# Interleaving the last recurrent segment with four gate/up products, moving weight loads to GpSimd's queue, and three small edits upstream

One Trainium2 chip, one core. The metric is the device time of one execution in microseconds, lower is better; medians of several runs are quoted. The page of a profile describes one execution only, and its span is a few microseconds shorter than that execution's device time.

## The reference, cut to what matters

```python
S, Dm, H, Dh, M, seg, F = 2048, 640, 32, 128, 8, 32, 1728
# A: 64 segments, one after the other
for s in range(64):
    h = concat([mem, xs])                    # 8 memory rows and 32 tokens
    q, k, v = h @ Wq, h @ Wk, h @ Wv          # 640 -> 32 heads x 128
    p = softmax(mask(q @ k.T * scale))
    o = (p @ v) @ Wo                          # back to 640
    mem = o[:, :M]                            # the next segment needs this
h1 = x + A(layernorm(x))
# B: gated feed-forward
out = h1 + (relu(ln(h1) @ W_gate) * (ln(h1) @ W_up)) @ W_down
```

The recurrence runs through `mem`, so the segments cannot overlap at will. The feed-forward works in four blocks of 512 tokens. Its first block (tokens 0 to 511) is ready long before segment 63 ends, so its gate and up products can fill TensorE in the last segment, once their weights have replaced Wq in SBUF.

## The kernel before

The kernel is written as one list of operations. Each names the tiles it reads and writes; a solver turns that into semaphore waits, and each engine is given its own operations in list order. These are the parts that matter (cuts are marked `# ...`):

```python
def load_gate_up():                     # called in segment 62, after the Q projection
    free = [("Wdone", 0)]               # Wq is free: gate and up lie over it
    dma(xn2T[0], xn2_d, ...)            # on SP's queue, 0.66 MB
    for n, (t, src) in enumerate(((Wg, B_W_gate), (Wu, B_W_up))):
        dma(t, src[..., 0:FM], r=free)                        # 2.13 MB
        dma(Wgu[:, :, n*FR:(n+1)*FR], src[..., FM:F], r=free) # 0.08 MB, rows of 128 bytes

for s in range(NSEG):
    project(a, ks, 1, (0, 1), BQ)       # K of this segment, in PSUM banks 0 and 1
    to_tok(BQ[0], 0, "act"); to_tok(BQ[1], 1, "dve")
    dma_t(KS, tokp[0])                  # DMA transpose on SP's queue
    trans_ox()                          # DMA transpose of the segment before: oT
    # ... late work
    project(a, ks, 0, (0, 1), (P0, P1)) # Q
    if s == NSEG - 2: load_gate_up()
    to_tok(P0, 2, "act"); to_tok(P1, 3, "dve")
    trans_q()                           # DMA transpose on SP's queue: QS
    # ... V projection, scores, exp
    v_riders(t0, nr)                    # small DMAs on GpSimd's queue: Vp -> Vr
    evac_q(QS, ("QS",), ..., "act")     # ACT waits here for QS
    # ... pv_mem
    if s % 4 == 1 and s >= 5:
        copy_op("dve", e0, oT[:, :, 0:M], ...)   # e0 is a view of `at`
    norm_om()
    # ... output projection wo_pass, to_act (next mem), pv_x, norm_x

# segment 63, after its scores:
wo_pass(T1); rows(T1, 0, s - 1)         # output projection of segment 62
gate_up(0, 0); pv_x(s, P0); norm_x(P0); trans_ox()
gate_up(0, 1); gate_up(0, 2); copy_oTe(s)
wo_pass(P2); rows(P2, 1, s)             # output projection of segment 63
gate_up(0, 3); woe_pass(P3, range(16))  # the rest, with the memory rows' sum
```

`gate_up(0, 0)` writes PSUM banks 0 and 2, `gate_up(0, 1)` banks 1 and 3. Bank 0 is also the first bank of the K projection. Both facts come back below.

## Time and profile before

| | before |
|---|---|
| device time, median of the 3 runs at hand for the prediction | 1147.25 us (1143.53 to 1151.35) |
| span of the profiled run | 1142.5 us |
| TensorE busy | 1065.7 us (93%) |
| an ordinary segment | 13.5 to 13.7 us |
| segments 33, 37, 41, 45 | 18.11, 15.45, 16.05, 14.83 us |
| segment 62 | 15.19 us |

TensorE is busy nearly all the time, so the table of busy shares says only that a gain must come from its holes. The prediction below shows the lines for those holes. One ruler is used throughout for the end of the recurrence: **the stretch**, from the start of the act_r cast that closes segment 61 to the end of the last matmul of the oTe product (`woe_pass`). Before, it runs from 910.28 to 966.50 us, so 56.22 us. What comes before it is "upstream"; what comes after it took 176.05 us in every profile of this study, so it plays no part.

### The profile page before, as it was taken

The page shows a single profiled execution, that of the slowest core. Times are in us where ns is not written, and L with a number is a line of the kernel's source. Part 1 is how long each engine was busy: PE and PEld are TensorE (multiplying, and loading weights), DVE is VectorE, ACT ScalarE, POOL GpSimd, SP SyncE. Part 2 cuts the span into 40 slices and gives each one's busy share as a digit, 9 for nine tenths or more (in the row PEclk, how much of TensorE's full clock was granted, in tenths as well). Part 3 has the DMA queues.
Part 4 walks back from the last instruction along what each step waited for, and adds up shares of the span by engine and source line. Part 5 has one row for each costly group of instructions (what it writes and reads, how often), then busy time and mean ns, then how long its engine had stood idle before and what let it go on. Part 6 is the DMA issues. An engine that isn't in the chain of part 4 may idle for free.

```text
span 1142.5 us, 55565 instructions
## 1 busy us (share of the span) xinstructions
PE 1065.7 (93%) x28016; PEld 507.1 (44%) x23471; DVE 593.9 (52%) x1477; ACT 353.3 (31%) x729; POOL 279.8 (24%) x567
## 2 busy tenths in 40 slices
PE   4589999999999999998999999999999957999998
PEld 2245545444444444544444444444444434443443
DVE  3245556565656565655655555565555522553532
ACT  2113333433333333342333333333333311221211
POOL 1013333333323232414132324142433300000000
PEclk9989999999999999999999999999999988999999
DMA  9944464635455455565656556454545384132100
GB/s 354 376 82 91 88 109 90 108 80 111 81 102 93 92 101 96 100 109 90 116 96 119 95 114 105 96 96 92 98 88 99 79 240 154 35 81 69 30 18 24
DMA packets 295416, 122.66 MB, mean 107 GB/s; under 512 B 269344, under 2 KB 284768, under 8 KB 295184
## 3 DMA queue, kind: packets, MB, share of 16 engines
q1 hardware_dynamic: 277328, 103.16, 41.5%
q0 software_dynamic: 17664, 15.94, 7.3%
q8 instruction: 202, 3.31, 1.2%
q14 instruction: 30, 0.25, 0.1%
q10 hardware_dynamic: 192, 0.01, 0.0%
HBM read 36.79 MB, written 7.21 MB: 39 GB/s over the span
## 4 chain that ended last, share of the span: by engine, by line
PE 83%; DMA 7%; DVE 4%; SPq 3%; issue 2%; ACT 0%; DVEq 0%
PE ps L410 23%; PE ps L388 22%; PE ps L627 14%; PE ps L998 10%; PE ps L1031 3%; PE ps L555 3%; SPq L356 3%; PE ps L641 3%; DMA Wo<-in_A_Wo_dram 3%; PE ps L592 2%; DVE TBf L539 2%; PE ps L439 2%; DMA xn_d<-at 1%; DMA Kr<-tok 1%; PE ps L607 1%
## 5 line engine op out<-in xcount | busy, mean ns | idle before, releaser
L410 PE MATMUL ps<-W,act_r 128*32 128x512 bf16 x4321 | 395.9, 383 | 15.7 <-DMA W<-in_A_Wq_dram 4.3
L388 PE MATMUL ps<-W,act_r 128*32 128x512 bf16 x3559 | 349.0, 379 | 0.0
L356 POOL DMA_DIRECT2D Vr<-Vp x376 | 187.5, 506 | 469.3 <-ACT Vp L450 294.6
L410 PEld LDWEIGHTS ps<-W,act_r 128*32 128x32 bf16 x4321 | 116.9, 97 | 272.8 <-issue 211.9
L450 ACT ACTIVATE tok<-ps 128x512 bf16<-128x512 f32 x191 | 110.2, 593 | 251.7 <-PE ps L388 232.9
L627 PE MATMUL ps<-Wo,oT 128*32 128x160 bf16 x8320 | 166.1, 239 | 16.3 <-DMA Wo<-in_A_Wo_dram 8.8
L627 PEld LDWEIGHTS ps<-Wo,oT 128*32 128x32 bf16 x8320 | 150.7, 100 | 43.0 <-DVE oT L452 24.4
L452 DVE CAST tok<-ps 128x512 bf16<-128x512 f32 x131 | 90.5, 691 | 146.5 <-PE ps L388 120.5
L410 PE MATMUL ps<-W,act_e 128*32 128x512 bf16 x900 | 91.3, 381 | 0.0
L388 PE MATMUL ps<-W,act_e 128*32 128x512 bf16 x900 | 90.7, 379 | 0.0
L450 ACT ACTIVATE Qr<-QS 128x512 bf16<-128x512 bf16 (+3 forms) x108 | 70.7, 681 | 44.3 <-DMA QS<-tok 43.9
L680 DVE TENSOR_TENSOR ox<-ps,rx 128x512 bf16<-128x512 f32 x128 | 82.5, 686 | 2.2
L356 POOL DMA_DIRECT2D attn_d<-wtok x64 | 46.6, 727 | 143.4 <-ACT wtok L450 143.4
L539 DVE STREAM_TRANSPOSE TBf<-ps 128x160 f32<-128x160 f32 x64 | 22.4, 350 | 92.9 <-PE ps L627 92.8
L1013 DVE TENSOR_TENSOR hT<-g,ps 128x512 bf16<-128x512 bf16 (+1 forms) x56 | 38.6, 689 | 58.8 <-PE ps L998 55.0
L998 PE MATMUL ps<-xn2T,Wu 128*128 128x512 bf16 x259 | 64.5, 379 | 0.1
L565 ACT ACTIVATE om<-ps 128x128 bf16<-128x128 f32 x63 | 17.5, 277 | 149.2 <-PE ps L555 149.2
L1031 PE MATMUL ps<-Wd,hT 128*128 128x320 bf16 (+1 forms) x240 | 63.3, 300 | 0.0
L998 PE MATMUL ps<-xn2T,Wg 128*128 128x512 bf16 x247 | 61.8, 379 | 1.3 <-issue 1.0
L1011 ACT ACTIVATE g<-ps 128x512 bf16<-128x512 f32 (+1 forms) x56 | 32.4, 592 | 94.5 <-PE ps L998 94.4
L452 DVE CAST Vp<-ps 128x512 bf16<-128x512 f32 x64 | 44.3, 692 | 32.6 <-PE ps L388 27.3
L388 PE MATMUL ps<-Wd,hT 128*128 128x320 bf16 x208 | 56.9, 299 | 0.0
(96 smaller groups left out, 1135.0 us busy)
## 6 DMA issues: line engine op xcount, KB each, us to landing
Vr<-Vp POOLq DMA_DIRECT2D x124, 48.8 KB, 2.0
W<-in_A_Wk_dram SPq DMA_DIRECT2D x2, 2560.0 KB, 12.8
W<-in_A_Wq_dram SPq DMA_DIRECT2D x2, 2560.0 KB, 25.7
W<-in_A_Wv_dram SPq DMA_DIRECT2D x2, 2560.0 KB, 27.6
Wo<-in_A_Wo_dram SPq DMA_DIRECT2D x2, 2560.0 KB, 28.1
xt<-in_A_x_dram SPq DMA_DIRECT2D x30, 160.0 KB, 3.6
Vr<-Vp POOLq DMA_DIRECT2D x128, 32.5 KB, 1.9
attn_d<-wtok POOLq DMA_DIRECT2D x64, 40.0 KB, 2.9
```

Of the source, the lines that this page charges most:

```text
L356: add(eng, lambda e: e.dma_start(dst, src), r=r, w=w, dma=True)
L388: return pe.add_instruction(mybir.InstMatmult(name=nc.get_next_instruction_name(), engine=mybir.EngineType.PE, ins=[pe.lower_ap(rhs), pe.l ...
L410: ins = pe.matmul(*a, start=(c == 0), stop=(c == DC - 1), skip_group_check=True)
L450: add("act", lambda a: a.activation(dst, src, ACTF.Copy), r=r, w=w)
L452: add("dve", lambda v: v.tensor_copy(dst, src), r=r, w=w)
L539: add("dve", lambda v: v.transpose(TBf[:].rearrange("p c t -> p (c t)"), src), r=[wkey], w=[("TBf",)])
L555: i = pe.matmul(bank((P0, P1)[g % 2])[p:p + (M if a else 32), 40 * k:40 * k + 40], lh, Qr[:, h, q, :], start=True, stop=True, skip_group_c ...
L627: i = pe.matmul(bank(bk)[32 * gg:32 * gg + 32, 0:160], oT[:, hb, :], w[:, gg], start=(hb == ORDER[0]), stop=(hb == ORDER[31]), skip_group_ ...
L680: add("dve", lambda v, kh=kh: v.tensor_tensor(ox[:, :, kh, :], src[:, :, kh, 0:128], ap(rx, kh, [[2, 4], [0, 128]]), ALU.mult), r=[B(b0 + ...
L998: ins = pe.matmul(bank(bk), w[:, c, lo:lo + 128], xn2T[par][:, c, :], start=(c == 0), stop=(c == DC - 1))
L1013: add("dve", lambda v: v.tensor_tensor(hT[par][lo:128, j, :], g1[gi][lo:128, :], bank(bu)[lo:128, :], ALU.mult), r=[B(bu), ("g1", gi)], w= ...
L1031: i = pe.matmul(*a, start=(j == 0), stop=(j == FC - 1), skip_group_check=True)
```

## The change

It intends four things: fill TensorE in segment 63 with four gate/up products placed between the recurrence's own steps; bring their weights through GpSimd's queue, so that the transposes on SP's queue need not stand behind 5 MB; stop DVE from waiting for a store (`oTn` instead of `at`); split the early LN2 statistics so that ACT is not held in front of an eviction. One more line extends the alignment of the output projections to segments 1 to 3: the kernel pads TensorE's instruction list so that these start at chosen places of a page, which it counts as 256 instructions (`PE_LINE`).

```diff
+    oTn = ar.alloc("oTn", [128, H, M], BF16)
...
-            copy_op("dve", e0, oT[:, :, 0:M], [("oT", "m")], [("at",)])
+            copy_op("dve", oTn[:, :, :], oT[:, :, 0:M], [("oT", "m")], [("oTn",)])
...
-            copy_op("dve", oTe[:, :, 0:M], e0, [("at",)], [("oTe", 0)])
+            copy_op("dve", oTe[:, :, 0:M], oTn[:, :, :], [("oTn",)], [("oTe", 0)])
...
-        wo_pass(T1, MARKS[s % 4] if s > 3 else None)
+        wo_pass(T1, MARKS[s % 4] if s > 0 else None)
...
-                row_stats(xt, ("xt",), 128)
+                row_moments(xt, ("xt",), 128)        # DVE half, where it was
             late.append(f)
+            late_q.append(lambda: row_rstd(128))     # ACT half, after the Q eviction
...   # xn2T, Wg, Wgu, Wu, Wgu in load_gate_up, then h, Wd, Wd: all eight
-            w=[("xn2", 0, u) for u in range(4)])
+            w=[("xn2", 0, u) for u in range(4)], eng="pool")
...   # segment 63
             to_v(P3, Vp, 1, ("Vp",), "dve")
+            if last:
+                to_v(P2, Vp, 0, ("Vp",), "act")
+                break
             scores(s)
...
+    gate_up(0, 0)
+    scores(s)
+    exp_x()
+    copy_oTe(s - 1)
+    mask_x()
+    gate_up(0, 1)
+    pv_x(s, P0)
+    norm_x(P0)
     wo_pass(T1)
     rows(T1, 0, s - 1)
-    gate_up(0, 0)
-    pv_x(s, P0)
-    norm_x(P0)
     trans_ox()
-    gate_up(0, 1)
     gate_up(0, 2)
+    gate_up(0, 3)
     copy_oTe(s)
     wo_pass(P2)
     rows(P2, 1, s)
-    gate_up(0, 3)
     woe_pass(P3, range(16))
```

More of the change, by code (lines that the diff above doesn't have):

```diff
@@ L359, in dma_t, with row_stats, row_moments @@
         add("sp", lambda e: e.dma_start_transpose(dst, src), r=r, w=w, dma=True)
-    def row_stats(src, skey, n):
+    def row_stats(src, skey, n, part=(0, 1)):
+        if 0 in part:
+            row_moments(src, skey, n)
+        if 1 in part:
+            row_rstd(n)
+    def row_moments(src, skey, n):
         for q in range(2):
@@ L365, in row_stats, with row_rstd @@
         add("dve", lambda v: v.bn_aggr(mv[0:n, :], st[0:n, :, :]), r=[("st", 0), ("st", 1)], w=[("mv",)])
+    def row_rstd(n):
         add("act", lambda a: a.activation(lv[0:n, :], mv[0:n, 1:2], ACTF.Ln, bias=eps[0:n, 0:1], scale=1.0),
@@ L808, in load_gate_up @@
         dma(xn2T[0][:, :, :], xn2_d[:, :, :], r=[("xn2_d", u) for u in range(4)] + [("Wdone", 0)],
-            w=[("xn2", 0, u) for u in range(4)])
+            w=[("xn2", 0, u) for u in range(4)], eng="pool")
         for n, (t, src) in enumerate(((Wg, B_W_gate), (Wu, B_W_up))):
-            dma(t[:, :, :], src.rearrange("(c p) f -> p c f", p=128)[:, :, 0:FM], r=free, w=[(("Wg", "Wu")[n],)])
+            dma(t[:, :, :], src.rearrange("(c p) f -> p c f", p=128)[:, :, 0:FM], r=free, w=[(("Wg", "Wu")[n],)], eng="pool")
             dma(Wgu[:, :, n * FR:(n + 1) * FR], src.rearrange("(c p) f -> p c f", p=128)[:, :, FM:F],
-                r=free, w=[("Wgu", n)])
+                r=free, w=[("Wgu", n)], eng="pool")
     PARTS = tuple((c,) for c in range(DC))
@@ L847, in extra_units @@
         return part, evac, (fin if j == 0 else None)
-    e0 = ap(at, 0, [[M, H], [1, M]])
     EARLY = (31, 35, 39, 43)
@@ L918, in build_kernel @@
             to_v(P3, Vp, 1, ("Vp",), "dve")
+            if last:
+                to_v(P2, Vp, 0, ("Vp",), "act")
+                break
             scores(s)
-            if not last:
-                exp_mem()
+            exp_mem()
             to_v(P2, Vp, 0, ("Vp",), "act")
             exp_x()
-            if last:
-                copy_oTe(s - 1)
-                mask_x()
-                break
             if nr:
@@ L1043, in build_kernel @@
     dma(h_rows[0][:, :, :], h_d[:, :].rearrange("(u p) d -> p u d", p=128), r=[("h_d", u) for u in range(4)] +
-        [("Wdone", 1)], w=[("h", 0, u) for u in range(4)])
+        [("Wdone", 1)], w=[("h", 0, u) for u in range(4)], eng="pool")
     dma(Wd[:, 0:FC - 1, :], B_W_down[0:FM, :].rearrange("(j p) d -> p j d", p=128),
-        r=[("Wdone", 1)], w=[("Wd", 0)])
-    dma(Wd[FR:128, FC - 1, :], B_W_down[FM:F, :], r=[("Wdone", 1)], w=[("Wd", 1)])
+        r=[("Wdone", 1)], w=[("Wd", 0)], eng="pool")
+    dma(Wd[FR:128, FC - 1, :], B_W_down[FM:F, :], r=[("Wdone", 1)], w=[("Wd", 1)], eng="pool")
     for i in range(4, 8):
```

## The prediction

> **What bounds the kernel now.** I read the page first, then the waits of TensorE, then the timeline where those waits are long. On the page:
>
> ```profile
> PE 1065.7 (93%) x28016; PEld 507.1 (44%) x23471; DVE 593.9 (52%) x1477; ACT 353.3 (31%) x729; POOL 279.8 (24%) x567
> PE 83%; DMA 7%; DVE 4%; SPq 3%; issue 2%; ACT 0%; DVEq 0%
> ```
>
> TensorE is the bound and the chain that ends last runs over it for 83%. Only the stretches where it stands can be won. The change touches no arithmetic on it, so I looked for its waits: first from 905 us to the end, then from 490 to 700 us.
>
> ```profile
> PE ps L555 <- DMA KS<-tok: 9.3, 1, 9.3
> PE ps L627 <- issue: 4.8, 2, 3.1
> ...
> DVE at L452 <- DMA xn_d<-at: 10.1, 4, 3.3
> ...
> PE ps L607 <- DVE om L600: 7.9, 4, 2.8
> ...
> PE ps L439 <- ACT tok L450: 1.9, 4, 0.5
> ```
>
> The columns are sum, times, longest. **The last segment** (63) waits 9.3 us for the transposed keys (KS). The timeline names what is behind it:
>
> ```profile
> 919.67 4.63 SPq L356 DMA_DIRECT2D Wgu<-in_B_W_up_dram  x1
> 924.40 7.16 SPq L359 DMA_TRANSPOSE QS<-tok  x1
> 935.45 0.63 ACT L450 ACTIVATE Qr<-QS 128x512 bf16<-128x512 bf16 x1 [15.79 <-DMA QS<-tok]
> 936.83 1.23 SPq L359 DMA_TRANSPOSE KS<-tok  x1
> 940.82 0.23 PE L555 MATMUL ps<-Qr,Kr 128*32 128x40 bf16 x4 [9.34 <-DMA KS<-tok]
> ```
>
> SP put 5 MB of gate and up weights on its queue from 916.48 us. The QS transpose of segment 62 comes behind them, ACT waits 15.8 us for it, so it evicts K of segment 63 late, so the KS transpose is issued at 936.83. TensorE had ended the V projection at 931.5. After 940.82 three more holes (3.1, 0.8 and 1.7 us, "issue") follow, in the output projections and in pv. The four gate/up products, two output projections and the oTe product end only at 966.5.
>
> **Segments 33, 37, 41, 45.** The copy of oT into `at` waits for the store of `at` to xn2_d:
>
> ```profile
> 513.68 0.62 SPq L356 DMA_DIRECT2D xn_d<-at  x1
> 517.49 0.23 DVE L452 COPY at<-oT 128x256 bf16<-128x256 bf16 x1 [3.35 <-DMA xn_d<-at]
> 518.32 0.29 PE L607 MATMUL ps<-ident,om 128*128 128x128 bf16 x2 [2.81 <-DVE om L600]
> ```
>
> The norm of `om` stands behind that copy on DVE, and TensorE behind the norm. The starts of the act_r cast (DVE, L540) mark the segments: those four last 18.11, 15.45, 16.05 and 14.83 us, while 49, 53 and 57 last 13.54, 13.62 and 13.60.
>
> [...] q1 is in order, so a transpose behind weights waits for them (7.16 us of issue against about 1.3 elsewhere). A change of queue removes the order, not the bytes. [...] The small ones here cost 0.5 to 0.7 us on POOL; no large one is in this trace. [...] clock 0.5 for 3.41 us from 518.8, from 921.57, and for 13.65 us from 935.22. [...] q8 shows 202 packets of 16 KB; the holes called "issue" end about 1.4 us after one lands (one from 943.61 to 944.62, PE goes on at 946.09).
>
> **The change part by part.**
>
> *Own buffer oTn.* It removes the wait for xn_d; the copy is as long (0.23 us). The four segments sum to 64.44 us; at 13.6 each they take 54.4. **Gain 10.0 us**: 7.9 of it the waits before L607, and about 1.7 the half clock that 2.8 us of idling brought on in segment 33 (its 128 matmuls of L627 took 3.90 us against 2.4). The later writer of `at` (ACT L855) still needs the store landed, but in segment 33 it would come at about 518, after the landing at 517.5.
>
> *Statistics split.* In segments 32, 36, 40, 44 ACT waits 1.69 us for the DVE aggregate before it evicts Q, and TensorE waits 0.47 us at L439 each time. With Ln and Exp behind the eviction this goes: **1.9 us**, by the waits view. The DVE half stays; its cast of Q is not late now (495.90, just after the projection).
>
> *Alignment from segment 1.* Counted in the program's instruction list before (64 ahead of it, as its PE_FIRST says), the output projections of segments 1, 2, 3 start at places 222, 209, 197 of a 256-instruction page; from segment 5 on at 158, 145, 133, 110 in turn. With a mark at segment 1 the pad is 192: 120 weight loads in its projections and 72 in the opening. Segments 2 and 3 then fall on 145 and 133 by themselves, and 4 on 110. Segment 3 lasts 16.26 us and has holes of 1.50 and 0.70 us; at the 13.6 of its successors it gains **2.6 us**. The 72 loads at about 0.1 us may delay the first transposes by 2 us; that vanishes in the wait for Wo at 54.1 to 60.6 us. Segment 1 (15.86) has no filler and idles for dependences: no gain.
>
> *The last segment*, in the times of the kernel before. POOL can issue at about 916.2, when Wq is free. Until Wu is in, 5.0 MB pass; from 917.5 to 933.3 q1 carried them at about 0.38 MB per us. Three transposes (1024 packets of about 19 ns, 1.2 us of all 16 engines each) now go between, and the x and attention rows that SP issues from about 932: estimate Wu in at 936. TensorE: first Wg product 931.5 to 932.6, then about 3.4 us idle; the second product, scores and the next pair are 1.1 + 0.5 + 2.2 us, plus 1.7 for one half-clock window: 941.5. The V riders of segment 62 now lie behind the weights in q0, so both copies into Vp wait for about 938 to 939; then copies, exp and masks make pv ready at about 941: just hidden. pv 0.5, output projection 2.4 plus one fetch hole of some 2.5 [...]: 947. Two gate/up pairs 4.3: 951.2, which hides the oT transpose (about 3 us, issued at 947). Output projection 2.4, oTe 2.4: **956**. Against 966.5: **gain 10.5 us**, of which the key wait is most, the rest fetch holes and half clock.
>
> Nothing after that changes: with Wd landing near 946, the first down product at 987 is far off. Sum: 10.0 + 1.9 + 2.6 + 10.5 = 25.0 us, less 0.7 for extra weight loads and small new waits: 24.3. 1147.25 - 24.3 = **1123 us**, ratio 0.979.
>
> **Rivals.** *A: the weights are late on GpSimd's queue.* [...] For it: in front of them TensorE has nothing else, and at 919.46 small q0 transfers got their first packets only at 923, beside q1 bulk. Against it: the bytes bound the load already, and POOL makes a 128-row store in 0.73 us. The last segment would gain 4 to 5, the time be 1129.
>
> *B: the wait moves instead of going.* Riders late in q0, oT waiting behind SP's x and attention loads, and a fetch hole in each output projection: the gain there would be 2 to 4 us, the time 1131. For it: all bulk, 9 MB, now lies in one stretch to about 947. Against it: the gate/up pairs stand in front of each user.
>
> *C: better than the sum.* Wu by 934.5, no half-clock window, no fetch hole: 4 to 6 us more, 1118. [...]
>
> *D: the oTn gain is smaller*, because ACT, DVE or the QS transpose (517.08 in segment 33) holds the same place. Against it: in segments 37, 41, 45 the excess over 13.6 (1.85, 2.45, 1.23) equals the L607 wait (1.73, 2.36, 1.04) within 0.2. It would cost 1 to 2 us.
>
> **Range and chances.** The three upstream parts, 14.5 us, I trust within 2. The last segment can give 2 to 15. So 1116 to 1132 holds eight in ten. Two per cent off is 1124.3, beside my 1123: 0.55 for faster, 0.44 same; slower would need the last segment to lose over 37 us: 0.01.
>
> **What would show it.** Right: segments 33, 37, 41, 45 at 13.5 to 13.7 us and no wait on xn_d before L607; no wait at L439 for ACT; segment 3 below 14; no KS wait, QS issued in 1.3 us; TensorE waiting for Wu at about 936 for 3 to 4 us; the oTe product ending 9 to 12 us nearer to the V projection's end than 35.0. Wrong: Wu landing after 940, TensorE waiting at pv for Vp or at the second output projection for oT by over 2 us, holes of over 4 us in the output projections, or a half clock lasting over two windows.

The figures of the profile before for what this says of the hardware:

- *Order on SP's queue.* The first packet of QS started at 932.0 us, 7.6 us after the start of its issue; by then all but 26 of the 1280 weight packets of 3328 bytes had started.
- *"The small ones" on POOL* are the transfers that GpSimd issues. They took 0.73 us each for the attention rows and about 0.5 us each for the V riders (1.97 us for the four from 919.46).
- *The load.* From 917.5 to 933.3 us the busy share of the DMA engines was 1.09.
- *The clock.* The granted clock was 0.5 in the three windows named. In the 3.41 us before each of them TensorE had been busy for 0.60, 1.53 and 0.00 us.
- *Instruction packets.* q8 brought 202 packets of 16 KB, and TensorE executed 28,016 matmuls and 23,471 weight loads: 255 for each packet, an estimate that takes all of them for TensorE's. Six of TensorE's "issue" holes were longer than 0.6 us; they ended 1.25 to 1.46 us after such a packet had landed.

## The result

The changed kernel takes 1134.23 us (median of 4, 1131.88 to 1138.43) beside 1146.92 us of the kernel before (median of 4). The ratio is 0.9891, with a 95% interval from 0.9846 to 0.9936. All ratios here are the mean time of one kernel's fast runs over that of the other's of the same rounds, so not quite the ratio of the medians. The change is a gain of about 1.1%, half of the 24 us that were predicted, and the time lies above the predicted range.

The profiled run of the changed kernel happens to be its slowest (1138.43 us; span 1136.7). In it the upstream part ends at 899.21 us instead of 910.28, but the stretch takes **61.43 us instead of 56.22**. The last segment lost 5 us in this run where 10.5 were to be won.

The upstream holes are gone. The waits of TensorE between 480 and 690 us in the changed kernel (sum, times, longest) no longer hold the store of `at`, the norm of `om` or ACT:

```profile
PE ps L636 <- issue: 0.6, 1, 0.6
PE ps L419 <- DVE act_r L549: 0.4, 2, 0.2
PE ps L419 <- ACT Vr L459: 0.2, 1, 0.2
```

The waits of TensorE from 895 to 965 us in the changed kernel:

```profile
PE ps L674 <- DVE Px L590: 6.1, 1, 6.1
PE ps L1005 <- ACT tok L459: 6.0, 1, 6.0
PE ps L616 <- DVE om L609: 3.5, 1, 3.5
PE ps L564 <- DMA KS<-tok: 2.2, 1, 2.2
PE ps L636 <- issue: 1.2, 1, 1.2
```

The one long wait for KS has become four waits, 17.8 us together; the "issue" holes have shrunk to 1.2 us. The timeline of the same run names what is behind each of the four:

```profile
905.41 1.38 SPq L360 DMA_TRANSPOSE QS<-tok  x1
...
911.19 0.23 DVE L461 COPY oTe<-oT 128x256 bf16<-128x256 bf16 x1 [3.12 <-DMA oT<-ox]
...
912.01 0.40 PE L616 MATMUL ps<-ident,om 128*32 128x128 bf16 x8 [3.54 <-DVE om L609]
...
927.67 0.69 DVE L461 CAST Vp<-ps 128x512 bf16<-128x512 f32 x1 [6.34 <-DMA Vr<-Vp]
927.81 0.63 ACT L459 ACTIVATE Qr<-QS 128x512 bf16<-128x512 bf16 x1 [19.29 <-DMA QS<-tok]
...
929.19 1.23 SPq L360 DMA_TRANSPOSE KS<-tok  x1
929.58 1.91 PE L1005 MATMUL ps<-xn2T,Wg 128*128 128x512 bf16 x4 [6.02 <-ACT tok L459]
...
935.09 0.20 PE L564 MATMUL ps<-Qr,Kr 128*32 128x40 bf16 x4 [2.22 <-DMA KS<-tok]
...
944.47 0.23 DVE L461 COPY oTe<-oT 128x256 bf16<-128x256 bf16 x1 [10.86 <-DMA oT<-ox]
...
945.68 0.32 PE L674 MATMUL ps<-Vr,Px 64*64 64x129 bf16 x4 [6.12 <-DVE Px L590]
```

SP issues QS at once now, in 1.38 us. But from its issue at 905.41 to ACT going on at 927.81 it takes 22.4 us; before, from 924.40, it was 11.05. The queue was left free and the transpose became slower. ACT stands 19.3 us for it, and what ACT should do next is to evict K of segment 63 from PSUM bank 0. The first gate product writes that bank, so it waits for ACT, with its weights already in. In segment 62 DVE stands for oT of segment 61, in front of the norm of `om`. In segment 63 DVE stands 10.9 us for oT of segment 62 (issued at 930.47, beside Wd), in front of the mask that pv needs.

The records of the single packets say why the transposes are slow. This table counts, in three separate microseconds, the packets that started on GpSimd's queue and on SP's in the changed kernel:

```text
us     weight packets (6656 bytes, 265 ns)   transpose packets (256 bytes, 18 ns)
914    52                                    52
918    61                                    63
922    64                                    66
```

The counts are nearly equal (two of the 64 have 4096 bytes). Spread evenly, the 1024 packets of a transpose are 64 for each of the 16 DMA engines. If each of them waits for one weight packet, as the counts suggest, that makes up to 64 x (265 + 18) ns = 18 us while weight packets last; the transpose's own share of the engines would be only 64 x 18 ns = 1.2 us. Both are estimates from these durations. In this run the weights ran out first. The packets of QS started from 911.6 to 926.6 us. Among them started 576 weight packets of 6656 bytes, 36 for each engine on average, and some 310 packets of QS came after the last weight packet (924.3). Before 911.6 QS stood in its own queue behind oT of segment 61, which had run beside the first of the loads (xn2T).

The two figures from issue, 22.4 and 11.05 us, overstate the loss, since before the change SP was held up in issuing the loads and QS itself. Counted from the issue of the first load, ACT went on with QS after 23.6 us in the changed kernel (904.25 to 927.81) and after 19.0 us before (916.48 to 935.45).

### The profile page after: what moved, and what is told of

The parts are those of the page before. It is cut to its first block, busy times and chain, and to the rows that moved or that the text cites. A ratio compares the mean times of both kernels' runs of the same rounds, so it can differ in the third digit from the quotient of the medians.

```text
span 1136.7 us, 55564 instructions
## 1 busy us (share of the span) xinstructions
PE 1067.6 (94%) x28016; PEld 511.8 (45%) x23471; DVE 592.9 (52%) x1477; ACT 352.8 (31%) x729; POOL 287.0 (25%) x575
## 4 chain that ended last, share of the span: by engine, by line
PE 83%; DMA 9%; DVE 3%; SPq 3%; issue 1%; ACT 1%; DVEq 0%; ACTq 0%
PE ps L419 24%; PE ps L397 23%; PE ps L636 13%; PE ps L1005 10%; DMA QS<-tok 5%; PE ps L1038 3%; PE ps L564 3%; SPq L357 3%; PE ps L650 3%; DMA Wo<-in_A_Wo_dram 3%; PE ps L601 2%; DVE TBf L548 2%; PE ps L448 2%; DMA oT<-ox 1%; DVE act_r L549 1%
## 5 line engine op out<-in xcount | busy, mean ns | idle before, releaser
L548 DVE STREAM_TRANSPOSE TBf<-ps 128x160 f32<-128x160 f32 x64 | 22.4, 349 | 98.0 <-PE ps L636 98.0
```

Of the source, the lines that this page charges most:

```text
L548: add("dve", lambda v: v.transpose(TBf[:].rearrange("p c t -> p (c t)"), src), r=[wkey], w=[("TBf",)])
```

## The experiments

All runs below gave correct results. "Upstream" is when the stretch starts. The two kernels with one look (e9, e10) have a single run each, of unknown state, and are not compared by time.

| run | median us | ratio to before (95%) | upstream | stretch |
|---|---|---|---|---|
| before | 1146 to 1147 | 1 | 910.28 | 56.22 |
| changed | 1134.23 | 0.9891 (0.9846 to 0.9936) | 899.21 | 61.43 |
| e1 upstream parts only | 1132.39 | 0.9883 (0.9856 to 0.9910) | 896.40 | 57.52 |
| e2 all loads on SP, new order | 1130.66 | 0.9873 (0.9846 to 0.9901) | 896.02 | 56.58 |
| e3 GpSimd's queue, old order | 1136.17 | 0.9921 (0.9893 to 0.9949) | 896.43 | 61.42 |
| e4 smaller packets | 1133.36 | 0.9901 (0.9868 to 0.9935) | 896.90 | 58.36 |
| e5 QS first | 1126.38 | 0.9816 (0.9786 to 0.9846) | 896.72 | 52.10 |
| e6 staged loads | 1119.84 | 0.9759 (0.9729 to 0.9789) | 896.06 | 46.54 |
| e7 GpSimd's queue, held until QS is in | 1130.96 | 0.9859 (0.9827 to 0.9891) | 896.06 | 56.75 |
| e8 oTn alone | 1135.27 | 0.9895 (0.9865 to 0.9924) | 900.93 | 57.27 |
| e9 loads by ACT, long rows | 1129.57, one look | | 897.27 | 54.53 |
| e10 loads by ACT, short rows | 1138.46, one look | | 899.85 | 60.81 |

**e1: upstream parts only.** The changed kernel, with the loads back on SP and the last segment in the old order.

```diff
-            ... eng="pool")        # all eight loads
+            ... )
-    gate_up(0, 0); scores(s); exp_x(); copy_oTe(s - 1); mask_x(); gate_up(0, 1); ...
+    (the order of the kernel before)
```

> The changed kernel with its last segment as before: loads on SP's queue and the old order; only oTn, the split statistics and the alignment stay. Theory T (the upstream parts gave all of the gain, and the last segment gave nothing or lost, because each 256-byte packet of a transpose waits for one weight packet of the other queue): 13 to 15 us less than before, 1131 to 1134, so the same as the changed kernel within 3 us; the last segment's KS wait is again 9 to 10 us. Rival R1 (upstream gained only about 8, as the profiled runs' segment starts say, and the last segment gave 4): 1138 to 1140. In the trace segments 33, 37, 41, 45 come to 13.5 to 14.1 and segment 3 to 13.8, and the extra 0.5 to 1 us that segments 8, 11, 12, 13 and 15 showed in the changed kernel's profile are not there.

Measured: 1132.39 us, ratio 0.9883. The three upstream parts alone give all of the gain; the changed kernel with its new last segment (0.9891) cannot be told from it. So the last segment's rebuilding gave nothing; by the profiles it lost 3.9 us of stretch (57.52 to 61.43). The waits of TensorE from 895 to 965 us are the old ones:

```profile
PE ps L564 <- DMA KS<-tok: 9.6, 1, 9.6
PE ps L636 <- issue: 6.1, 2, 4.5
```

Segments 8 to 15 took 109.6 us together here, 108.8 before and 112.5 in the changed kernel's profile. They run the same code in e1 and in the changed kernel, so the 3 us seem to belong to that one slow execution and not to the change. Segment 37 took 14.98 us here and 15.47 in e10; it is 13.6 to 13.8 with the same code in the changed kernel, e2, e5 and e6, so this too varies from one execution to the next.

**e2: all loads on SP, the new order kept.**

```diff
-            ... eng="pool")        # all eight loads
+            ... )
```

> The changed kernel with all eight loads on SP's queue again; the new order of the last segment stays. Theory T: the QS transpose of segment 62 stands behind 5 MB in order, as before, and lands about 19 us after the first load's issue, against 23.6 us in the changed kernel; oT of segment 61 is issued ahead of the loads and no longer waited for; TensorE then has the first gate/up pair to do while KS comes. So 5 to 8 us faster than the changed kernel, 1126 to 1129. Rival R2 (the queue is what helps and the order is what hurts): slower than the changed kernel, 1137 or more.

Measured: 1130.66 us, ratio 0.9873, a stretch of 56.58. It was not slower, so the order does no harm, but the 5 to 8 us did not come: the intervals of e2 and of the changed kernel overlap. TensorE's longest waits:

```profile
PE ps L636 <- issue: 5.7, 3, 3.5
PE ps L1005 <- ACT tok L459: 5.5, 1, 5.5
PE ps L419 <- issue: 2.3, 1, 2.3
```

The first gate product cannot use the time in which KS is missing, because it waits for the eviction of K out of bank 0, and ACT stands before that eviction, waiting for QS. My expectation had the same hole as my prediction: it looked at when the weights are in, and not at who holds the bank. The other 8 us are holes called "issue", which my expectation did not count either.

**e3: GpSimd's queue with the old order.**

```diff
-    gate_up(0, 0); scores(s); exp_x(); copy_oTe(s - 1); mask_x(); gate_up(0, 1); ...
+    (the order of the kernel before)
```

> The upstream parts with the loads on GpSimd's queue and the old order of the last segment. Theory T: QS again lands over 20 us after the first load, the oT wait of about 3 us in segment 62 is there, and scores stand behind KS with nothing before them: 3 to 6 us slower than the kernel with the upstream parts alone, about 1137. Rival R2: faster than that kernel by 3 us or more.

Measured: 1136.17 us and a stretch of 61.42, 3.9 us longer than e1's. The seven runs lie between 1132.46 and 1140.71, those of e1 from the same rounds between 1130.74 and 1132.77. TensorE's two longest waits in this stretch are both for transposes:

```profile
PE ps L564 <- DMA KS<-tok: 10.7, 1, 10.7
PE ps L636 <- DMA oT<-ox: 9.4, 1, 9.4
```

With e1, e2 and the changed kernel this makes a square: on SP's queue the new order is worth 0.9 us of stretch, on GpSimd's queue 0.0; the move to GpSimd's queue costs 3.9 and 4.9. These are single profiles, but they agree with the medians in sign. By itself, the move to the other queue is a loss of some 4 us. It is what is left of two opposite effects: from 895 to 965 us the "issue" holes come to about 8 us in e1 and e2, with the loads on SP's queue, and to 1.5 and 2.3 us in e3 and the changed kernel, with the loads on GpSimd's. So the waits for transposes cost more than the 4 us. Why the holes are shorter there is not shown.

**e4: smaller packets.** In the changed kernel the packets of GpSimd's loads have 6656 bytes for Wg and Wu (two rows of 3328) and 5120 for Wd (four rows of 1280), where SP's had one row each in the kernel before (3328 and 1280). Here the rows of the column pieces are 1024 bytes, and the packets came out at 4096. The loads of the W tiles have packets of that size too: 3840 of them, 160 ns each.

```diff
-            dma(t[:, :, :], src[..., 0:FM], r=free, w=[(("Wg", "Wu")[n],)], eng="pool")
+            for m, (lo, hi) in enumerate(((0, 512), (512, 1024), (1024, 1536), (1536, FM))):
+                dma(t[:, :, lo:hi], src[..., lo:hi], r=free, w=[(("Wg", "Wu")[n], m)], eng="pool")
```

> The changed kernel with the gate and up weights loaded in column pieces (512, 512, 512, 128), same bytes, same queue. In the changed kernel a packet of these loads carries 6656 bytes (two rows) and takes 265 ns; if packets are filled to 4096 bytes, as those of the other loads seem to be, they take about 165 ns. Theory T (one packet each by turns): the time from issue to landing of QS falls from 22.4 us to about 12 to 15, because each of its 64 packets per engine waits 165 and not 265 ns; the kernel gains 3 to 7 us over the changed one, 1127 to 1131. Rival R3 (the transposes get a share of bytes or are last in rank, whatever the packet): QS lands when the weights are through, as now, 22 us, and the time is that of the changed kernel.

Measured: 1133.36 us, and QS takes 20.6 us from issue (903.59) to ACT going on (924.21), against 22.4. Inconclusive by itself, and my expectation was badly worked out: it forgot that oT of segment 61 is in the same queue ahead of QS and takes 64 turns as well. In the changed kernel Wg and Wu are 640 packets of 6656 bytes, 40 per engine on average, and in e4 they would be some 80 by the bytes. Two transposes come to 128 turns per engine, so they run out of weight packets first. The packet records do show the turns: 71 to 80 weight packets and 82 to 98 transpose packets in each busy microsecond, at 187 ns. e9 and e10 were made to settle it.

**e9 and e10: the same loads from ACT's queue, with long and with short rows.** There a packet is one row: 3328 bytes in e9, 1024 in e10. ACT issues the loads after its eviction of Q, so that QS runs beside them.

```diff
-            ... eng="pool")        # the five loads of load_gate_up
+            ... eng="act")         # e10: in the column pieces of e4 as well
-                if s == NSEG - 2: load_gate_up()
                 to_tok(P0, 2, "act")
+                if s == NSEG - 2: load_gate_up()
```

> A measurement of the disputed cost, not a candidate: the five gate and up loads of the changed kernel issued by ACT (its own queue, in which a packet is one row of 3328 bytes, 131 ns), behind ACT's eviction of Q, so that QS of segment 62 and the weights share the engines from two queues. The time itself means little, since ACT stands while it issues. Turn theory: each engine moves 64 of QS's packets, one per weight packet, so QS needs about 64 x (131 + 18) = 9.5 us while long rows are in flight, and the counts of packets of the two queues are equal in each microsecond. Share of bytes: 1.5 to 3 us. Last in rank: only when the weights are through, 14 us or more.

> As e9, with the weights in column pieces of 512, 512, 512 and 128, so that a packet is 1024 bytes, about 50 ns. Turn theory: QS in about 64 x (50 + 18) = 4.4 us, half of e9's or less, at the same bytes and the same rank. Share of bytes or last in rank: as in e9.

Packets that started in one full microsecond, from the records of each run:

```text
run      weight packet        us     weight packets   transpose packets
changed  6656 bytes, 265 ns   922    64               66
e4       4096 bytes, 187 ns   913    80               92
e9       3328 bytes, 131 ns   908    109              110
e10      1024 bytes,  46 ns   914    287              284
```

At each of these four packet lengths the two queues moved nearly equal numbers of packets, so the transpose moved faster the shorter the other queue's packets were: 66, 92, 110, 284 per us. And the transposes do not wait for the end of the weights: the last packet of QS starts at 916.2 in e9 and 916.5 in e10, while weights go on until 923.6 and 926.3. That rules out the theory of a lower rank, and a share of bytes is ruled out by the counts. The durations did not come out as I expected. The packets of QS took 4.7 us in e9 (911.6 to 916.2; expected 9.5) and 5.0 us in e10 (911.4 to 916.5; expected 4.4), so e10 was not the quicker one. In e9 QS met only 395 of the long packets, and 640 of 128 bytes (Wgu): 1035 for its own 1024, so over the whole of it too the turns were one for one. In e10 it met 1158 packets of 1024 bytes, but both queues moved fewer packets in parts of the first 3 us; what held them there I did not find out.

**e5: QS first.** e2 with one move.

```diff
-                if s == NSEG - 2: load_gate_up()
                 to_tok(P0, 2, "act"); to_tok(P1, 3, "dve")
                 ...
                 if nr: trans_q()
+                if s == NSEG - 2: load_gate_up()
```

> The kernel of e2 (all loads on SP, new order) with one move: the five gate and up loads are issued after the QS transpose of segment 62, not before it. Theory T, with what the traces added (ACT holds the K evictions, and with them PSUM bank 0 of the first gate product, while it waits for QS): QS lands in 3 us, ACT is free, TensorE waits only for Wu; scores wait little. From the last act_r cast of segment 61 to the end of the oTe product it is 56.2 us in the kernel before, 61.4 in the changed one, 56.6 in e2; here 43 to 47. So 10 to 13 us faster than e2, 1118 to 1121. Rival R4 (TensorE would have waited for the 5 MB anyway, and QS only hides it): 53 to 56 us, the time within 3 us of e2.

Measured: 1126.38 us, ratio 0.9816, stretch 52.10. It is 4.3 us faster than e2 by the medians, less than the 10 to 13 expected: it lies between the turn theory (43 to 47 us of stretch) and rival R4 (53 to 56), nearer to R4. What is left:

```profile
PE ps L1005 <- DMA Wu<-in_B_W_up_dram: 2.9, 1, 2.9
PE ps L636 <- issue: 2.5, 2, 1.8
PE ps L419 <- issue: 2.3, 1, 2.3
PE ps L636 <- DMA oT<-ox: 2.2, 1, 2.2
PE ps L564 <- DMA KS<-tok: 1.4, 1, 1.4
```

ACT's wait is gone: QS took 4.7 us from issue to use, beside 22.4 in the changed kernel and 11.05 before. KS and oT still stand behind weights in SP's queue, and two long "issue" holes (2.3 and 1.8 us) are there while bulk loads run.

**e6: staged loads.** As e5, but with the first 1024 columns of gate and up only; the other columns, the x and attention rows, h and Wd are issued behind the last oT transpose.

```diff
+    EARLY_J = 8
     def load_gate_up():
         dma(xn2T[0], xn2_d, ...)
+        load_columns(0, EARLY_J * 128, 0)
...
     trans_ox()
+    load_rest()            # columns 1024 to 1663, both Wgu
+    for i in range(4, 8): ln2_load(i)
+    dma(h_rows[0], ...); dma(Wd, ...); dma(Wd, ...)
     gate_up(0, 2)
```

> As e5, but only the first 1024 columns of gate and up (3.3 MB with xn2T) go behind QS of segment 62; the rest, the x and attention rows, h and Wd go behind the last oT transpose. Theory T: KS and oT of segment 63 find an empty queue, the first gate product starts at the end of the V projection, and no transpose waits: 38 to 42 us for the same stretch, 1113 to 1117, the fastest. If a later wait comes (gate product 8 for its columns, down for Wd) it shows after the oTe product and the tail is longer than the 176.05 us that all runs so far have. Rival R4: no faster than e2.

Measured: **1119.84 us, ratio 0.9759**, the fastest kernel of the study, 1.3% under the changed one by the medians, with no load on GpSimd's queue. The stretch is 46.54 us, against 38 to 42 expected. Timeline of e6:

```profile
912.89 1.47 SPq L360 DMA_TRANSPOSE KS<-tok  x1
...
918.62 1.25 PE L1015 MATMUL ps<-xn2T,Wg 128*128 128x512 bf16 x5
...
920.88 0.20 PE L564 MATMUL ps<-Qr,Kr 128*32 128x40 bf16 x4
...
937.90 0.85 PE L636 MATMUL ps<-Wo,oT 128*32 128x160 bf16 x37 [4.45 <-issue]
```

The gate product and the scores start with no wait at all. (The queue was not quite empty, as the expectation had it: KS still stood behind the first loads, and its packets started at 916.1. The gate product and the up product hid that.) The difference to the expectation is two "issue" holes, 2.3 us in the K projection and 4.45 us in the last output projection; each falls in a time of bulk loads, and each ends 1.4 to 1.6 us after a 16 KB packet of instructions has landed (before, the holes of 3.1, 0.8 and 1.7 us in the last segment ended 1.5, 1.3 and 1.3 us after one). That the fetch is their cause is inferred from this. I left them there. The tail was 176.04 us, so no later wait came in their place.

**e7: GpSimd's queue, the loads held until QS of segment 62 has landed.**

```diff
-        dma(xn2T[0], xn2_d, r=[..., ("Wdone", 0)], ..., eng="pool")
+        dma(xn2T[0], xn2_d, r=[..., ("Wdone", 0), ("QS",)], ..., eng="pool")   # and called after trans_q
```

> The changed kernel (loads on GpSimd's queue) with the five loads held until QS of segment 62 has landed. Theory T: QS and oT(61) are not starved, so no 3 us hole in segment 62, but KS and oT of segment 63 fall among the weight packets and take their 64 turns each: KS lands only about when the weights are through. 44 to 50 us for the stretch, 1119 to 1125: better than the changed kernel by 9 or more, and not better than e5. Rival R5 (a software queue slows transposes as such, even at their ends): over 55 us.

Measured: 1130.96 us, stretch 56.75. The first half came out: QS is issued at 902.29 and ACT goes on with it at 907.11, so here the loads on GpSimd's queue did not slow the transpose that ran before them. The second half was worse than expected: KS of segment 63 falls into the weights.

```profile
913.16 1.29 SPq L360 DMA_TRANSPOSE KS<-tok  x1
914.50 14.28 SPq L360 DMA_TRANSPOSE oT<-ox  x1
925.75 2.32 PE L1005 MATMUL ps<-xn2T,Wu 128*128 128x512 bf16 x5 [5.62 <-DMA Wu<-in_B_W_up_dram]
933.78 0.23 PE L564 MATMUL ps<-Qr,Kr 128*32 128x40 bf16 x4 [5.71 <-DMA KS<-tok]
```

From its issue to the scores KS took 20.6 us, nearly as long as QS in the changed kernel, and the scores began 8 us after Wu was in (925.75). Its packets started from 916.8 to 932.6, with 771 weight and h packets of 5120 or 6656 bytes among them. I had it landing with the weights and did not count that h and Wd follow them at once in the same queue, so the turns went on. The loads also began later: TensorE stood 4.0 us more before its first gate product (918.59), which the waits view calls "issue"; Wg had landed just then, 10.3 us after its issue at 908.24. The nearest kernel to compare is e5, which has the same order of products and all five loads behind QS, but on SP's queue: 52.10 us of stretch and 1126.38 us, so here too GpSimd's queue was not the better place.

**e8: oTn alone, on the kernel before.**

```diff
+    oTn = ar.alloc("oTn", [128, H, M], BF16)
-            copy_op("dve", e0, oT[:, :, 0:M], ...)
+            copy_op("dve", oTn[:, :, :], oT[:, :, 0:M], ...)
-            copy_op("dve", oTe[:, :, 0:M], e0, ...)
+            copy_op("dve", oTe[:, :, 0:M], oTn[:, :, :], ...)
```

> The kernel before with the oTn buffer alone. 8 to 10 us faster than before, 1136 to 1139; segments 33, 37, 41, 45 at 13.6 to 14.2; segment 3 still at 16 and segments 32, 36, 40, 44 still at 13.9 to 14.4; the last segment as before. If another wait took the place of the xn_d one, under 4 us.

Measured: 1135.27 us, ratio 0.9895: most of the upstream gain is this one buffer. Segments 33, 37, 41 and 45 take 13.68, 13.65, 13.66 and 13.62 us, 9.8 us less in sum than before; segment 3 is still at 16.40. The timeline in segment 33 shows the copy going on while the store, which it used to wait for, is under way, and TensorE's only wait from 485 to 695 us is the one that the split statistics remove (two views of e8, in this order):

```profile
513.31 0.62 SPq L357 DMA_DIRECT2D xn_d<-at  x1
514.70 0.22 DVE L453 COPY oTn<-oT 128x256 bf16<-128x256 bf16 x1
```

```profile
PE ps L440 <- ACT tok L451: 1.9, 4, 0.5
```

## Why the prediction was wrong

**Own buffer oTn: right.** Predicted 10.0 us; in e8 the four segments gave 9.8 us. In the other profiles with this buffer they gave 6.7 (e10) to 9.8 us (e6). The half clock of segment 33 went with the wait: in the changed kernel the granted clock was full from 78.65 to 911.5 us.

**Statistics split: right.** Predicted 1.9 us. Segments 32, 36, 40 and 44 took 56.52 us before, 54.83 in the changed kernel, 53.86 in e1 and 55.77 in e8, which lacks the split. So 1.9 us by e8 against e1, and the wait at the Q eviction is in e8 and not in the other two. The ten profiles with the split spread from 53.65 to 55.10 us, so single profiles give between 0.7 and 2.1 us; that the pair e8 and e1 gives exactly 1.9 is partly luck.

**Alignment: right.** Predicted 2.6 us in segment 3: 16.26 us became 13.77 in the changed kernel, 13.54 in e1, and is 16.40 in e8 without it. The opening did not grow: the first act_r cast starts at 12.07 us, 12.14 before.

The sum of these, 14.5 us, is what e1 gave by the upstream time (910.28 to 896.40, so 13.9) and about what it gave by the medians.

**The last segment: wrong.** Predicted 10.5 us; it gave nothing (e1 against the changed kernel), and by the profiles the stretch grew from 56.2 to 61.4. The prediction placed its end at 956, 45.7 us after the start of the stretch. Step by step:

- *Weights in at 936*, 25.7 us into the stretch: right as a number. Wu, issued at 906.55, landed 18.2 us later, at about 924.8, 25.5 us in. The hit is partly luck, since two errors met in it. The rate before was misread: 5.06 MB in the 15.8 us from 917.5 to 933.3 are 0.32 MB per us and not 0.38. And the prediction made room for the x and attention rows, which SP issued only at 932.32, when the weights were in. Rival A, late weights, is ruled out: GpSimd needed 0.88 to 0.90 us to issue each of the large loads.
- *"Three transposes (1024 packets of about 19 ns, 1.2 us of all 16 engines each) now go between"*: this is the step that failed. I charged the transposes to the weights, at their own 1.2 us, and took it that they land as usual. In these traces the two queues moved their packets nearly one for one (66 of the transpose and 64 of the weights in microsecond 922), so it was the transposes that paid, about one large packet for each of their own while large packets lasted. From issue to use QS took 22.4 us, oT of segment 61 some 7 (904.01 to 911.19, beside xn2T), oT of segment 62 14.0 (930.47 to 944.47, with 471 packets of 5120 bytes among its own, 29 for each engine on average). I had reckoned with a sharing of bytes.
- *"First Wg product 931.5 to 932.6"*: failed as a consequence. Bank 0 was held until ACT, standing for QS, had evicted K; the product began 30.4 us into the stretch, and 21.2 had been predicted.
- *"V riders ... just hidden"*: the copy into Vp did wait for the riders until 927.67 (28.5 us in), as worked out (28 to 29). It cost nothing, since ACT and QS were later.
- *The fetch hole*: 2.5 us predicted, 1.2 us found as an "issue" hole in the changed kernel.
- *The half clock*: one window of 3.4 us was reckoned with; the granted clock was 0.5 for 6.8 us from 911.5, for 3.4 us each from 928.57 and 935.39, and for 6.8 us from 942.22. In the 3.41 us before these, TensorE had been busy for 0.38, 0.00, 1.19 and 0.75 us; before 935.39 its longest wait was 2.2 us. So the extra waits seem to have cost a second time: the first output projection in the stretch took 4.46 us instead of 2.4. How long a wait brings the half clock on is not shown.

Rival B had named this outcome ("the wait moves instead of going", oT behind other loads) and given it 1131. Its mechanism was off as well: it feared SP's queue order. The argument against it, that the gate/up pairs stand in front of each user, failed because a pair that waits itself for a PSUM bank or for ACT (6.0 us in the changed kernel) hides nothing.

What stays open: what makes the holes called "issue" so long beside bulk loads on SP's queue (2.3 and 4.45 us in e6), and whether another placing of the page boundaries would remove them.

## What to carry to other kernels

In these runs a second DMA queue ended the waiting in line (QS was issued in 1.38 us instead of 7.16), but two busy queues moved nearly equal numbers of packets (66 and 64 in a microsecond), so a transfer of many small packets (a transpose) beside one of few large packets ran at the pace of the large ones: QS took 22.4 us from issue to use. Put the urgent small transfer first and send only as much bulk as fits before the next one; here that (e6) was worth 14 us more than moving the bulk to another queue (the changed kernel). And before counting a filler product as free, look at who still holds its PSUM bank, and what that engine waits for.
